# Attention inside a fused kernel: the value product with values stationary, and probabilities divided ahead of their transposes

## The chip, the cores and the metric

The kernel runs on one core of a Trainium2 chip. The metric is the device time of one execution in microseconds (us); lower is better. Engines are named as the profile names them: PE (matrix products; PEld is its weight loads), DVE, ACT and POOL (element-wise work), SP (issues most DMAs).

## What is computed

Three layers run one after another: chunked attention over 4 batches, 8 heads and 768 positions with 64 features per head; a two-layer network of width 2048; RMS normalisation and a gated two-layer network of width 1536. Only the attention is touched:

```
for each chunk of 32 queries (16 positions of left and 8 of right context, 8 memory slots):
    scores = (1/8) * q_chunk @ k_full.T          # k_full: 8 memory + up to 56 keys
    a = exp(scores - max);  a = a / (sum(a) + 1e-9)
    out_chunk = a @ v_full
x = out, tokens by 512 features (8 heads x 64)   # goes into the network after it
```

## The kernel before

The 3072 tokens are cut into 24 attention tiles of 128 tokens (four chunks of 32). Each tile goes through five steps, a PE part followed by the engine work that takes its result out of PSUM:

- **a** (L433, L445): 4 PE transposes of the queries (L438) and 4 of a key tile (L395); ACT and DVE copy them out.
- **b** (L453, L466): 32 score products, each 64 rows by 32 columns of the PE array, with 64 key columns moving (L458). In the trace each of these float32 products stands as two pairs of weight load and matmul, so a tile shows 64. DVE takes maxima (L471) and subtracts them (L472), ACT takes the exponentials (L477).
- **c** (L486, L495): 4 transposes of the probabilities (L490), copied out by ACT (L497).
- **d** (L501, L516): 32 value products (L506): the transposed probabilities are the stationary operand (32 queries), the values move, 64 features and a 65th column of ones, whose result is the sum. DVE adds the epsilon (L519), takes the reciprocal (L520) and multiplies (L522).
- **e** (L528, L535): the result has queries on partitions, and the next layer wants features there: 4 transposes (L532), copied by ACT (L539) into `xb`, which holds 384 tokens.

Scores and values share the PSUM pair `bkp`; all transposes rotate over two banks. `att_list` (L544) writes the steps of six tiles as a list with one step of lag between the letters: in each round e of tile t-4, d of t-3, c of t-2, b of t-1, a of t. The first list (tiles 0 to 5) runs at the start, with the conversion of the first weights (L202 to L216) put between its pieces; as soon as tile 2 has passed its last step (L976), `x_split` makes the first operands T out of `xb` and the first main products (L639 to L641, 384 columns each) begin to be put in. The lists for tiles 6 to 23 are spread over the slots between main products (`slots`, L990). Within this program order a scheduler fixes the order on each engine, and each engine then runs its own order strictly.

The values are loaded by SP (L379) as rows of 64 floats into `vw`, whose rows are 65 floats apart; raw weights for the conversion are loaded by POOL's queue (L149) into two buffers, so that POOL waits there until DVE has read the older one (L210). POOL also copies memory values (L385) and, later, adds for the main products (L669).

Of the kernel before, what the change touches and what calls it, by code (L numbers as in the profile page):

```python
# [8 lines left out]
F32 = mybir.dt.float32  # L9
# [4 lines left out]
ALU = mybir.AluOpType  # L14
AX = mybir.AxisListType

EPS_RMS = 1e-6
EPS_SUM = 1e-9
# [11 lines left out]
def tile_kernel(  # L30
# [15 lines left out]
    nc = tc.nc  # L46
    pin = tc.keep_in_program_order
    B, H, S, D = q.shape
    NMEM = mem_k.shape[2]
# [4 lines left out]
    NP = H // 2  # L54
# [269 lines left out]

    rot = [0]
    qn, kn, vn, ktw, qT, pt, pT = {}, {}, {}, {}, {}, {}, {}
    vw = [atp.tile([128, NP, 4, D + 1], F32, tag=f"vw{u}", name="vw") for u in range(2)]
    kw2 = [atp.tile([128, NP, 4, 64], F32, tag=f"kw{u}", name="kw") for u in range(2)]

    SMALL = [(2 * a + e, c) for a in range(NP) for c in range(4) for e in range(2)]  # L330

    def bank():
        rot[0] = (rot[0] + 1) % 2
        return bk[4 + rot[0]]
# [26 lines left out]
    def load_v(t):  # L361
        b, i = divmod(t, SPB)
        s0 = 128 * i
        vt = vw[t % 2]
        vn[t] = vt
        for h2 in range(2):
            p0 = 64 * h2
            if i < 2:
                src = mem_v[b].rearrange("(a e) s d -> e s a d", e=2)[h2]
                nc.sync.dma_start(out=vt[p0:p0 + NMEM, :, 3, 0:D], in_=src)  # L370
            for c in range(4):
                lo = 16 if i == 0 and c == 0 else 0
                hi = 48 if i == SPB - 1 and c == 3 else 56
                src = bass.AP(
                    v.tensor,
                    v.offset + ((b * H + h2) * S + s0 + 32 * c + lo - 16) * D,
                    [[D, hi - lo], [2 * S * D, NP], [1, D]],
                )
                nc.sync.dma_start(out=vt[p0 + NMEM + lo:p0 + NMEM + hi, :, c, 0:D], in_=src)  # L379

    def mem_v_copy(t):
        if t % SPB < 2:
            vt = vn[t]
            for p0 in (0, 64):
                nc.gpsimd.tensor_copy(  # L385
                    vt[p0:p0 + NMEM, :, 0:3, :],
                    vt[p0:p0 + NMEM, :, 3:4, :].to_broadcast([NMEM, NP, 3, D + 1]),
                )

    def k_pe(b, i):  # L390
# [75 lines left out]
    def att_b1(t):  # L466
        i = t % SPB
        ps = st_b.pop(t)
        mx = at2.tile([128, 2, NP], F32, tag="mx", name="mx")
        p = at1.tile([128, NP, 2, 64], F32, tag="p", name="p")  # L470
        nc.vector.reduce_max(mx, ps, axis=AX.X)  # L471
        nc.vector.tensor_tensor(  # L472
            p.rearrange("p a e k -> p e a k"), ps,
            mx.unsqueeze(3).to_broadcast([128, 2, NP, 64]), op=ALU.subtract
        )
        p = p.rearrange("p a e k -> p (a e) k")
        nc.scalar.activation(p, p, ACTF.Exp, scale=scale)  # L477
        if i == 0:
            nc.vector.memset(p[0:32, :, 8:24], 0.0)
        if i == SPB - 1:  # L480
            nc.vector.memset(p[96:128, :, 56:64], 0.0)
        pt[t] = p

    st_c, st_d, st_e, xs_t, xb = {}, {}, {}, {}, {}

    def att_c(t):  # L486
        p = pt.pop(t)
        pp = bank().rearrange("p (a s) -> p a s", a=NP)
        for a in range(NP):
            nc.tensor.transpose(  # L490
                pp[:, a, :], p[:, 2 * a:2 * a + 2, :].rearrange("s h d -> s (h d)"), ident
            )
        st_c[t] = pp

# [5 lines left out]

    def att_d(t):  # L501
        w, vt = pT.pop(t), vn[t]
        px = bk2[:, :, 0:NP * (D + 1)].rearrange("p e (a d) -> p e a d", a=NP)
        for h, c in SMALL:
            p0 = 64 * (h % 2)
            nc.tensor.matmul(  # L506
                px[32 * c:32 * c + 32, h % 2, h // 2, :],
                w[p0:p0 + 64, h // 2, 32 * c:32 * c + 32],
                vt[p0:p0 + 64, h // 2, c, :],
                tile_position=(p0, 32 * c),  # L510
            )
        st_d[t] = px
        if t + 2 < TSUB:
            load_v(t + 2)

    def att_d1(t):  # L516
        px = st_d.pop(t)
        sm = at2.tile([128, 2, NP], F32, tag="sm", name="sm")
        nc.vector.tensor_scalar_add(sm, px[:, :, :, D], EPS_SUM)  # L519
        nc.vector.reciprocal(sm, sm)  # L520
        x = at1.tile([128, NP, 2, D], F32, tag="x", name="x")
        nc.vector.tensor_tensor(  # L522
            x.rearrange("p a e d -> p e a d"), px[:, :, :, 0:D],
            sm.unsqueeze(3).to_broadcast([128, 2, NP, D]), op=ALU.mult
        )
        xs_t[t] = x

    def att_e(t):  # L528
        x = xs_t.pop(t)
        px = bank().rearrange("p (a s) -> p a s", a=NP)  # L530
        for a in range(NP):
            nc.tensor.transpose(px[:, a, :], x[:, a, :, :].rearrange("p e d -> p (e d)"), ident)  # L532
        st_e[t] = px

    def att_e1(t):  # L535
        n, r = divmod(t, NSUB)
        if r == 0:
            xb[n] = atx.tile([128, KC, N], F32, tag="xb", name="xb")
        nc.scalar.copy(xb[n][:, :, 128 * r:128 * r + 128], st_e.pop(t))  # L539

    att_ops = {"a": att_a, "a1": att_a1, "b": att_b, "b1": att_b1,
               "c": att_c, "c1": att_c1, "d": att_d, "d1": att_d1, "e": att_e, "e1": att_e1}

    def att_list(j):  # L544

        out = []
        t0 = TPP * j
        for s in range(TPP + 4):
            for op, lag in (("e", 4), ("d", 3), ("c", 2), ("b", 1), ("a", 0)):
                t = t0 + s - lag  # L550
                if t0 <= t < t0 + TPP:
                    if op == "a" and t % SPB == 0:
                        out.append([(att_a0, t)])
                    out.append([(att_ops[op], t), (att_ops[op + "1"], t)])
        return out
# [372 lines left out]
    make_identity(nc, ident)  # L928
    for x in vw:
        nc.gpsimd.memset(x, 0.0)  # L930
        nc.gpsimd.memset(x[:, :, :, D:D + 1], 1.0)
    nc.gpsimd.memset(ones, 1.0)
    nc.scalar.copy(ones_r, ones)

# [28 lines left out]
    for n, piece in enumerate(first):  # L963
        if n == 2:
            load_v(0)
        if n == 6:
            load_v(1)
        if n == 4:
            load_q(3)
        if n == 4:  # L970
            cv_prefetch(0)
        for fn, t in piece:
            fn(t)
        if n >= 4:
            cv_upto(CV_START * (n + 1 - 4) // (len(first) - 4))
        if piece[0] == (att_e, NSUB - 1):  # L976
            for half in range(2):
                x_split(0, half)
            heads, at_head = [unit(0, i) for i in range(NHEAD)], n
        elif n - at_head in HEADS:  # L980
            if next(heads[0], "end") == "end":
                heads.pop(0)
                next(heads[0])
# [304 lines left out]
```

## Time and profile before

| | |
|---|---|
| median of 3 runs | 1166.92 us (1166.48 to 1168.05) |
| the profiled execution | 1167.72 us, its span 1166.0 us |
| PE busy / PE weight loads busy | 1140.7 us (98%) / 1005.2 us (86%) |
| DVE / ACT / POOL busy | 823.8 / 629.2 / 183.4 us |
| chain that ended last | PE 75%, DMA 9%, DVE 8%, ACT 5% |

The attention lies in the first 310 us of the span. A busy PE in this profile is counted from a matmul's start to its modelled end, so bursts of small products count as busy whatever they do. In the trace's rows a line number is that of the kernel before, and a tile's name (`bkp`, `T`, `x`) is the program's.

### The profile page before, as it was taken

The page shows a single profiled execution, that of the slowest core. Times are in us where ns is not written, and L with a number is a line of the kernel's source. Part 1 is how long each engine was busy: PE and PEld are TensorE (multiplying, and loading weights), DVE is VectorE, ACT ScalarE, POOL GpSimd, SP SyncE. Part 2 cuts the span into 40 slices and gives each one's busy share as a digit, 9 for nine tenths or more (in the row PEclk, how much of TensorE's full clock was granted, in tenths as well). Part 3 has the DMA queues.
Part 4 walks back from the last instruction along what each step waited for, and adds up shares of the span by engine and source line. Part 5 has one row for each costly group of instructions (what it writes and reads, how often), then busy time and mean ns, then how long its engine had stood idle before and what let it go on. Part 6 is the DMA issues. An engine that isn't in the chain of part 4 may idle for free.

```text
span 1166.0 us, 22910 instructions
## 1 busy us (share of the span) xinstructions
PE 1140.7 (98%) x9052; PEld 1005.2 (86%) x9052; DVE 823.8 (71%) x1254; ACT 629.2 (54%) x1008; POOL 183.4 (16%) x165
## 2 busy tenths in 40 slices
PE   5899999999999999999999999999999999999998
PEld 4799999999999888888878778888888888999998
DVE  3655798844745876866776765967896857888873
ACT  4566666543645896677775443544454423444441
POOL 3011231311132311010011121110211111000000
PEclk8899999999999999999999999999999999999999
DMA  9989799898488774594599398999898889655421
GB/s 195 187 219 224 191 300 260 240 297 284 170 302 290 255 225 144 188 354 157 195 375 409 123 349 316 355 407 359 312 363 356 329 283 319 180 160 145 145 91 37
DMA packets 213276, 294.20 MB, mean 252 GB/s; under 512 B 104240, under 2 KB 160560, under 8 KB 204336
## 3 DMA queue, kind: packets, MB, share of 16 engines
q1 hardware_dynamic: 210864, 284.34, 73.5%
q0 software_dynamic: 2304, 8.39, 2.3%
q8 instruction: 71, 1.16, 0.4%
q14 instruction: 37, 0.30, 0.1%
HBM read 181.80 MB, written 110.89 MB: 251 GB/s over the span
## 4 chain that ended last, share of the span: by engine, by line
PE 75%; DMA 9%; DVE 8%; ACT 5%; issue 2%; POOL 0%; SPq 0%; ACTq 0%; DVEq 0%; POOLq 0%
PE bk L639 13%; PE bk L640 13%; PE bk L641 13%; DMA s<-g_scratch 4%; PE bk L912 4%; PE bk L914 4%; PE bk L913 4%; PE bk L755 3%; PE bk L756 3%; PE bk L754 3%; DVE T L154 2%; PE bkp L639 2%; PE bkp L640 2%; PE bkp L641 2%; PE bkp L506 2%
## 5 line engine op out<-in xcount | busy, mean ns | idle before, releaser
L639 PE MATMUL bk<-T,w 128*128 128x384 f32 (+1 forms) x860 | 315.6, 369 | 1.3 <-ACT c L657 1.0
L640 PE MATMUL bk<-T,w 128*128 128x384 f32 (+1 forms) x860 | 311.2, 362 | 0.0
L641 PE MATMUL bk<-T,w 128*128 128x384 f32 (+1 forms) x860 | 307.4, 361 | 0.0
L639 PEld LDWEIGHTS bk<-T,w 128*128 128x128 f32 x860 | 162.0, 189 | 21.0 <-ACT c L657 1.3
L640 PEld LDWEIGHTS bk<-T,w 128*128 128x128 f32 x860 | 161.9, 188 | 16.5 <-DVE T L154 0.3
L641 PEld LDWEIGHTS bk<-T,w 128*128 128x128 f32 x860 | 161.5, 188 | 15.8
L912 PE MATMUL bk<-w,T 128*128 128x256 f32 x396 | 112.1, 283 | 0.2 <-ACT T L153 0.2
L913 PE MATMUL bk<-w,T 128*128 128x256 f32 x396 | 112.0, 283 | 0.0
L914 PE MATMUL bk<-w,T 128*128 128x256 f32 x396 | 111.9, 283 | 0.0
L755 PE MATMUL bk<-T,w 128*128 128x512 f32 x276 | 107.5, 390 | 0.5 <-DVE T L154 0.5
L756 PE MATMUL bk<-T,w 128*128 128x512 f32 x276 | 107.1, 389 | 0.0
L754 PE MATMUL bk<-T,w 128*128 128x512 f32 x276 | 105.8, 389 | 0.0
L669 POOL TENSOR_TENSOR v<-c,v 128x512 f32<-128x512 f32 x36 | 54.1, 1503 | 291.7 <-DVE c L665 259.0
L665 DVE TENSOR_TENSOR c<-bk,c 128x512 f32<-128x512 f32 (+2 forms) x72 | 43.0, 598 | 54.5 <-PE bk L641 41.9
L912 PEld LDWEIGHTS bk<-w,T 128*128 128x128 f32 x396 | 76.0, 192 | 0.5 <-ACT T L153 0.4
L913 PEld LDWEIGHTS bk<-w,T 128*128 128x128 f32 x396 | 76.0, 192 | 0.0
L914 PEld LDWEIGHTS bk<-w,T 128*128 128x128 f32 x396 | 75.9, 192 | 0.0
L649 ACT COPY c<-bk 128x512 f32<-128x512 f32 (+2 forms) x72 | 36.9, 514 | 69.1 <-PE bk L641 25.3
L154 DVE TENSOR_TENSOR T<-s,T 128x1024 fp32r<-128x1024 f32 (+1 forms) x50 | 62.5, 1258 | 15.2 <-ACT T L153 15.1
L782 ACT ACTIVATE s<-s 128x1024 f32<-128x1024 f32 x44 | 46.4, 1059 | 31.3 <-DMA s<-g_scratch 31.2
L755 PEld LDWEIGHTS bk<-T,w 128*128 128x128 f32 x276 | 51.8, 188 | 11.6 <-DVE T L154 0.9
L756 PEld LDWEIGHTS bk<-T,w 128*128 128x128 f32 x276 | 51.8, 188 | 10.8
(228 smaller groups left out, 2284.6 us busy)
## 6 DMA issues: line engine op xcount, KB each, us to landing
T<-nt_scratch SPq DMA_DIRECT2D x35, 1024.0 KB
g_scratch<-g SPq DMA_DIRECT2D x64, 384.0 KB
s<-g_scratch SPq DMA_DIRECT2D x46, 512.0 KB
h_scratch<-s SPq DMA_DIRECT2D x36, 512.0 KB
w<-wg SPq DMA_DIRECT2D x10, 1792.0 KB
wg<-w SPq DMA_DIRECT2D x30, 512.0 KB
raw<-in_moe_w_out_dram SPq DMA_DIRECT2D x28, 512.0 KB
nt_scratch<-T SPq DMA_DIRECT2D x14, 1024.0 KB
```

The source lines that it names most:

```text
L154: keep((eng or nc.vector).tensor_tensor(lo, src, hi.bitcast(F32), op=ALU.subtract))
L639: nc.tensor.matmul(ps, whi, xh, start=first and kk == 0, stop=False, **more)
L640: nc.tensor.matmul(ps, whi, xl, start=False, stop=False, **more)
L641: nc.tensor.matmul(ps, wlo, xh, start=False, stop=kk == 1, **more)
L669: nc.gpsimd.tensor_tensor(c22, u3, z5, op=ALU.add)
L754: nc.tensor.matmul(ps, ahi, bhi, start=start, stop=False)
L755: nc.tensor.matmul(ps, ahi, blo, start=False, stop=False)
L756: nc.tensor.matmul(ps, alo, bhi, start=False, stop=stop)
L782: nc.scalar.activation(x, g, self.act)
L912: nc.tensor.matmul(ps, t[:, 0, f], w[:, 0], start=first and f == 0, stop=False, **more)
L913: nc.tensor.matmul(ps, t[:, 0, f], w[:, 1], start=False, stop=False, **more)
L914: nc.tensor.matmul(ps, t[:, 1, f], w[:, 0], start=False, stop=f == HG - 1, **more)
```

## The change

The value product swaps its operands. Values become stationary, in halves of 32 features (64 keys by 32 features), and the transposed probabilities move, 32 queries at a time. The result leaves with features on partitions, the layout that `xb` wants, so step e (its 4 transposes, its pass through PSUM) is gone and ACT copies the product straight into `xb`. A product now has 32 moving columns instead of 65, and a tile has 64 of them instead of 32. The column of ones is gone, and rows of `vw` are 64 floats apart. The sum is taken from the probabilities by DVE, and the probabilities are divided ahead of step c: on DVE for tiles 0 to 5, on POOL after that. A list has 25 pieces instead of 31.

```diff
-    vw = [atp.tile([128, NP, 4, D + 1], F32, tag=f"vw{u}", name="vw") for u in range(2)]
+    vw = [atp.tile([128, NP, 4, D], F32, tag=f"vw{u}", name="vw") for u in range(2)]
+    NFIRST = 6
+    VALUES = [(a, c, cols) for a in range(2) for c in range(4) for cols in range(4)]
...
     def att_b1(t):
...
-        pt[t] = p
+        sm = at2.tile([128, H], F32, tag="sm", name="sm")
+        nc.vector.reduce_sum(sm, p, axis=AX.X)
+        nc.vector.tensor_scalar_add(sm, sm, EPS_SUM)
+        nc.vector.reciprocal(sm, sm)
+        pn = at1.tile([128, NP, 2, 64], F32, tag="x", name="x")
+        mul = nc.vector if t < NFIRST else nc.gpsimd
+        mul.tensor_tensor(
+            pn.rearrange("p j r k -> p r j k"), p.rearrange("p (r j) k -> p r j k", r=2),
+            sm.rearrange("p (r j) -> p r j", r=2).unsqueeze(3).to_broadcast([128, 2, NP, 64]),
+            op=ALU.mult,
+        )
+        pt[t] = pn
...
     def att_d(t):
         w, vt = pT.pop(t), vn[t]
-        px = bk2[:, :, 0:NP * (D + 1)].rearrange("p e (a d) -> p e a d", a=NP)
-        for h, c in SMALL:
-            p0 = 64 * (h % 2)
-            nc.tensor.matmul(
-                px[32 * c:32 * c + 32, h % 2, h // 2, :],
-                w[p0:p0 + 64, h // 2, 32 * c:32 * c + 32],
-                vt[p0:p0 + 64, h // 2, c, :],
-                tile_position=(p0, 32 * c),
-            )
+        px = bk2[:, :, 0:256].rearrange("p e (a s) -> p e a s", a=2)
+        for a, c, cols in VALUES:
+            for e in range(2):
+                o = 32 * cols
+                j, d0 = 2 * a + cols // 2, 32 * (cols % 2)
+                p0 = 64 * e
+                nc.tensor.matmul(
+                    px[o:o + 32, e, a, 32 * c:32 * c + 32],
+                    vt[p0:p0 + 64, j, c, d0:d0 + 32],
+                    w[p0:p0 + 64, j, 32 * c:32 * c + 32],
+                    tile_position=(p0, o),
+                )
...
-    def att_e(t):
...
-    def att_e1(t):
...
-        nc.scalar.copy(xb[n][:, :, 128 * r:128 * r + 128], st_e.pop(t))
+        nc.scalar.copy(
+            xb[n].rearrange("p (e a) n -> p e a n", e=2)[:, :, :, 128 * r:128 * r + 128], st_d.pop(t)
+        )
...
-        for s in range(TPP + 4):
-            for op, lag in (("e", 4), ("d", 3), ("c", 2), ("b", 1), ("a", 0)):
+        for s in range(TPP + 3):
+            for op, lag in (("d", 3), ("c", 2), ("b", 1), ("a", 0)):
...
-        if piece[0] == (att_e, NSUB - 1):
+        if piece[0] == (att_d, NSUB - 1):
             for half in range(2):
                 x_split(0, half)
```

What the scheduler makes of it is shown at three places. In the rows of the change the lines are those of the changed kernel: L397 keys, L440 queries, L460 scores, L503 probability transposes, L522 values, L638 to L640 main products.

PE in the start of the program, from the keys of tile 5 (`kn`) to the first main product; before:

```order
L395 MATMUL bk_87<-ident,kn 128x128 x4
L458 MATMUL bkp<-kw,qT 32x64 x32
L532 MATMUL bk_86<-ident,x 128x128 x4
L506 MATMUL bkp<-vw,pT 32x65 x32
L490 MATMUL bk_87<-ident,p 128x128 x4
L438 MATMUL bk_86<-ident,qn 128x128 x4
L458 MATMUL bkp<-kw,qT 32x64 x32
L395 MATMUL bk_87<-ident,kn 128x24 x4
L532 MATMUL bk_86<-ident,x 128x128 x4
L506 MATMUL bkp<-vw,pT 32x65 x32
L490 MATMUL bk_87<-ident,p 128x128 x4
L639 MATMUL bk_82<-T,w 128x384
```

The same place with the change:

```order
L397 MATMUL bk_86<-ident,kn 128x128 x4
L522 MATMUL bkp<-pT,vw 32x32 x64
L503 MATMUL bk_87<-ident,x 128x128 x4
L440 MATMUL bk_86<-ident,qn 128x128 x4
L460 MATMUL bkp<-kw,qT 32x64 x32
L638 MATMUL bk_82<-T,w 128x384
L639 MATMUL bk_82<-T,w 128x384
```

The first main product now follows the scores of tile 4 directly; the values of tile 3, the transposes of tile 4 and the last, short key tile, which stood ahead of it, come behind.

DVE after the scores of tile 0 (`mx` maxima, `p` probabilities); before:

```order
L471 TENSOR_REDUCE mx<-bkp 128x8
L472 TENSOR_TENSOR p<-bkp,mx 128x2x4x64
L404 COPY kw<-bk_87 128x4x24
L479 MEMSET p 32x8x16
L471 TENSOR_REDUCE mx<-bkp 128x8
L472 TENSOR_TENSOR p<-bkp,mx 128x2x4x64
```

With the change:

```order
L473 TENSOR_REDUCE mx<-bkp 128x8
L474 TENSOR_TENSOR p<-bkp,mx 128x2x4x64
L406 COPY kw<-bk_87 128x4x24
L481 MEMSET p 32x8x16
L485 TENSOR_REDUCE sm<-p 128x8
L486 TENSOR_SCALAR sm<-sm 128x8
L487 RECIPROCAL sm<-sm 128x8
L490 TENSOR_TENSOR x<-p,sm 128x2x4x64
L473 TENSOR_REDUCE mx<-bkp 128x8
```

Four operations stand between the exponentials of a tile and its transposes, and ahead of the maxima of the next tile.

POOL where tiles 6 to 8 come (`raw` raw weights, `vw` values); before:

```order
L149 DMA raw<-in_moe_w_in_dram 128x2x512 x4
L385 COPY vw<-vw 8x4x195
L149 DMA raw<-in_moe_w_in_dram 128x2x512
L385 COPY vw<-vw 8x4x195 x3
L149 DMA raw<-in_moe_w_in_dram 128x2x512 x8
```

With the change:

```order
L149 DMA raw<-in_moe_w_in_dram 128x2x512 x4
L387 COPY vw<-vw 8x4x192 x2
L149 DMA raw<-in_moe_w_in_dram 128x2x512 x2
L387 COPY vw<-vw 8x4x192 x2
L490 TENSOR_TENSOR x<-p,sm 128x2x4x64
L149 DMA raw<-in_moe_w_in_dram 128x2x512 x2
L490 TENSOR_TENSOR x<-p,sm 128x2x4x64
L149 DMA raw<-in_moe_w_in_dram 128x2x512
L490 TENSOR_TENSOR x<-p,sm 128x2x4x64
```

The products with the reciprocal alternate with the issues of raw loads, which wait for a free buffer.

## Rows read from the trace of the kernel before

**Rows 1.** Stretches: us, busy by engine (instructions), granted clock, DMA share, GB/s.
```profile
0.00:40.00 40.00, 25.14 (x584) 18.25 (x584) 17.83 (x37) 20.99 (x40) 10.24 (x20) 0.83 0.93 193
40.00:50.00 10.00, 8.64 (x151) 7.65 (x136) 6.48 (x12) 5.76 (x11) 0.72 (x1) 0.83 0.97 193
50.00:70.00 20.00, 19.09 (x334) 17.04 (x319) 11.87 (x22) 12.52 (x25) 5.04 (x6) 1.00 0.87 193
70.00:220.00 150.00, 150.00 (x2282) 140.11 (x2270) 117.94 (x226) 95.63 (x186) 31.27 (x37) 1.00 0.88 237
230.00:310.00 80.00, 80.00 (x1143) 74.67 (x1142) 42.54 (x81) 33.94 (x64) 8.66 (x8) 1.00 0.78 251
```

**Rows 2.** Groups by line: busy us, mean ns of one | idle before, who ended it.
```profile
L669 POOL TENSOR_TENSOR v<-c,v 128x512 f32<-128x512 f32 x36 | 54.1, 1503 | 291.7 <-DVE c L665 259.0 <-ACT v L657 14.5 <-ACT s L747 12.0
...
L458 PE MATMUL bkp<-kw,qT 64*32 64x64 f32 x1536 | 24.4, 234 | 0.8 <-DVE x L522 0.7
L506 PE MATMUL bkp<-vw,pT 64*32 64x65 f32 x1536 | 22.9, 229 | 2.3 <-DMA vw<-in_v_dram 1.0 <-POOL vw L385 1.0 <-DVE p L472 0.2
...
L471 DVE TENSOR_REDUCE mx<-bkp 128x8 f32<-128x512 f32 x24 | 16.5, 688 | 25.0 <-PE bkp L458 24.9
...
L532 PE MATMUL bk<-ident,x 128*128 128x128 f32 x96 | 15.2, 283 | 2.0 <-ACT qT L449 1.9
...
L520 DVE RECIPROCAL sm<-sm 128x8 f32<-128x8 f32 x24 | 4.8, 201 | 0.7
```

**Rows 3.** Timeline of PE around lone result transposes: start us, us, what, count.
```profile
252.50 0.33 PE L641 MATMUL bk<-T,w 128*128 128x384 f32 x1
252.67 0.34 PE L639 MATMUL bk<-T,w 128*128 128x384 f32 x1
252.85 0.60 PE L532 MATMUL bk<-ident,x 128*128 128x128 f32 x4
...
253.47 0.33 PE L641 MATMUL bk<-T,w 128*128 128x384 f32 x1
```

**Rows 4.** Timeline of PE around a lone values burst.
```profile
196.75 0.34 PE L641 MATMUL bk<-T,w 128*128 128x384 f32 x1
197.02 0.86 PE L506 MATMUL bkp<-vw,pT 64*32 64x65 f32 x64
...
198.09 0.34 PE L640 MATMUL bk<-T,w 128*128 128x384 f32 x1
```

**Rows 5.** The same view at 39 us: a scores burst at half the clock.
```profile
39.07 1.06 PE L458 MATMUL bkp<-kw,qT 64*32 64x64 f32 x64
```

**Rows 6.** A slice of that burst: us, busy (instructions), granted clock, DMA share, GB/s.
```profile
39.40:39.60 0.20, 0.20 (x35) 0.50 1.01 257
```

**Rows 7.** PE, started from 197.0 to 197.3: matmuls of the burst of Rows 4.
```profile
197.02 0.48 PE L506 MATMUL bkp<-vw,pT 64*32 64x65 f32 x33
```

**Rows 8.** PE weight loads of that burst that started from 197.4 to 197.6.
```profile
197.40 0.31 PEld L506 LDWEIGHTS bkp<-vw,pT 64*32 64x32 f32 x25
```

**Rows 9.** Timeline of PE ahead of the first main product.
```profile
40.85 0.66 PE L532 MATMUL bk<-ident,x 128*128 128x128 f32 x4 [0.37 <-ACT qT L449]
...
42.85 0.87 PE L506 MATMUL bkp<-vw,pT 64*32 64x65 f32 x50 [0.79 <-DMA vw<-in_v_dram]
...
44.42 1.63 PE L639 MATMUL bk<-T,w 128*128 128x384 f32 x4
```

**Rows 10.** Timelines of ACT and PE at tile 15: exponentials, then transposes.
```profile
186.17 0.63 ACT L477 ACTIVATE p<-p 128x512 f32<-128x512 f32 x1
...
186.85 0.66 PE L490 MATMUL bk<-ident,p 128*128 128x128 f32 x4
```

**Rows 11.** DMA queue of SP, 2.5:4.2 us, queries and keys: packets, MB, share of 16 engines.
```profile
q1 hardware_dynamic: 1248, 0.31, 80.9%
```

**Rows 12.** DMA queue of SP, 48:53 us, values: packets, MB, share of 16 engines.
```profile
q1 hardware_dynamic: 3431, 0.85, 124.4%
```

**Rows 13.** DMA queue of SP, 41.2:45.6 us, mostly values: packets, MB, share of 16 engines.
```profile
q1 hardware_dynamic: 1900, 0.46, 50.9%
```

More of the change, by code (lines that the diff above doesn't have):

```diff
@@ L368, in load_v @@
             if i < 2:
-                src = mem_v[b].rearrange("(a e) s d -> e s a d", e=2)[h2]
-                nc.sync.dma_start(out=vt[p0:p0 + NMEM, :, 3, 0:D], in_=src)
+                src = mem_v[b].rearrange("(e a) s d -> e s a d", e=2)[h2]
+                nc.sync.dma_start(out=vt[p0:p0 + NMEM, :, 3, :], in_=src)
             for c in range(4):
@@ L375, in load_v @@
                     v.tensor,
-                    v.offset + ((b * H + h2) * S + s0 + 32 * c + lo - 16) * D,
-                    [[D, hi - lo], [2 * S * D, NP], [1, D]],
+                    v.offset + ((b * H + NP * h2) * S + s0 + 32 * c + lo - 16) * D,
+                    [[D, hi - lo], [S * D, NP], [1, D]],
                 )
-                nc.sync.dma_start(out=vt[p0 + NMEM + lo:p0 + NMEM + hi, :, c, 0:D], in_=src)
+                nc.sync.dma_start(out=vt[p0 + NMEM + lo:p0 + NMEM + hi, :, c, :], in_=src)
     def mem_v_copy(t):
@@ L386, in mem_v_copy @@
                     vt[p0:p0 + NMEM, :, 0:3, :],
-                    vt[p0:p0 + NMEM, :, 3:4, :].to_broadcast([NMEM, NP, 3, D + 1]),
+                    vt[p0:p0 + NMEM, :, 3:4, :].to_broadcast([NMEM, NP, 3, D]),
                 )
@@ L481, in att_b1 @@
             nc.vector.memset(p[96:128, :, 56:64], 0.0)
-        pt[t] = p
-    st_c, st_d, st_e, xs_t, xb = {}, {}, {}, {}, {}
+        sm = at2.tile([128, H], F32, tag="sm", name="sm")
[10 more added lines that the diff above has]
+        pt[t] = pn
+    st_c, st_d, xb = {}, {}, {}
     def att_c(t):
@@ L490, in att_c @@
             nc.tensor.transpose(
-                pp[:, a, :], p[:, 2 * a:2 * a + 2, :].rearrange("s h d -> s (h d)"), ident
+                pp[:, a, :], p[:, a].rearrange("s h d -> s (h d)"), ident
             )
@@ L516, in att_d1 @@
     def att_d1(t):
[L517 to L526, printed above, removed]
-    def att_e(t):
[L529 to L533, printed above, removed]
-    def att_e1(t):
         n, r = divmod(t, NSUB)
@@ L538, in att_e1 @@
             xb[n] = atx.tile([128, KC, N], F32, tag="xb", name="xb")
-        nc.scalar.copy(xb[n][:, :, 128 * r:128 * r + 128], st_e.pop(t))
+        nc.scalar.copy(
+            xb[n].rearrange("p (e a) n -> p e a n", e=2)[:, :, :, 128 * r:128 * r + 128], st_d.pop(t)
+        )
     att_ops = {"a": att_a, "a1": att_a1, "b": att_b, "b1": att_b1,
-               "c": att_c, "c1": att_c1, "d": att_d, "d1": att_d1, "e": att_e, "e1": att_e1}
+               "c": att_c, "c1": att_c1, "d": att_d, "d1": att_d1}
     def att_list(j):
@@ L930, in tile_kernel @@
         nc.gpsimd.memset(x, 0.0)
-        nc.gpsimd.memset(x[:, :, :, D:D + 1], 1.0)
     nc.gpsimd.memset(ones, 1.0)
```

## The prediction

> **What bounds the kernel now.** Read first the table of stretches [rows 1]. From 70 to 220 us PE is busy 150.00 of 150.00 us, from 230 to 310 us 80.00 of 80.00, while DVE has 117.94 of 150. There a microsecond of PE work, added or removed, is a microsecond of the total, and other engines matter only where they make PE wait. The start is different: PE is busy 25.14 of the first 40 us, 8.64 of the next 10 and 19.09 of the 20 after them, 17.1 us of idle in all, with DMA at 0.93 and 0.97; the granted clock averages 0.83 there, 2.4 GHz with stretches of 1.2. There the order of loads and the length of the chain decide. Then the groups by line [rows 2], for prices; then timelines around single pieces [rows 3 to 10], because busy time of overlapped bursts doesn't tell what a burst costs PE's stream. The profiled execution took 1167.7 us, 0.8 above the median of 1166.9; I work out differences and put them on the median.
>
> **Step e goes (24 times).** Around a lone set of result transposes, main products start at 252.50, 252.67, then 252.85 for the transposes, and 253.47 for the second product behind them [rows 3]. An ordinary step is 0.17; from 252.67 to 253.47 there are two steps and the transposes, so a set costs 0.80 - 0.34 = 0.46 us. 24 x 0.46 = 11.0 us less.
>
> **Step d doubles its instructions (24 times).** A lone burst of 64 stands between the products at 196.75 and 198.09 [rows 4]: 1.34 - 0.34 = 1.00 us now. With the change it is 128 pairs, each with 32 moving columns instead of 65. No row shows such a burst, so I bound its extra cost.
> Near the bottom: is the pace set by columns? A scores burst of the same 64 took 1.06 us [rows 5] in a slice where the clock was 0.50, the level of 1.2 GHz [rows 6], against 0.86 at full clock [rows 4]. Halving the clock added 0.20, so at most about 0.20 of the 0.86 hangs on columns. A matmul's own run is 0.23 [rows 2]. The remaining 0.86 - 0.20 - 0.23 = 0.43 goes with the number of instructions and doubles: +0.43. (If pace went by columns alone it would be +0, but these rows speak against it.)
> From the pace: the first 33 matmuls of the burst cover 0.48 us [rows 7], or 32 starts in 0.48 - 0.23 = 0.25, 8 ns each. The other 31 need 0.86 - 0.48 = 0.38, 12 ns each: +0.78 for 64 more at that pace. Within that slower half the weight loads run 25 in 0.2 us, 8 ns each [rows 8], and only its two ends are slow. I take 0.52 (64 at 8.2), since a longer burst has the same ends once. 24 x 0.52 = 12.5 us more; bounds 10.3 and 18.7.
> [...]
>
> **The start.** Before the change, the first main product stands at 44.42 [rows 9], behind the result transposes of tile 2 (40.85), the values of tile 3, whose rest waited for a load until 42.85, and the transposes of tile 4. In the new order it stands right behind the scores of tile 4, which end at 39.07 + 1.06 = 40.1 [rows 5]: up to 4.3 us earlier. Not all of it is gain. What PE no longer does ahead of it (d of tile 3 at 1.00; c of tile 4, three sets of e and a short key tile, as five sets of transposes at 0.46: 3.3 us) it partly does later, and the three value bursts that stay are 0.52 longer, so work ahead falls by about 1.7 and idle by about 2.6. I take 2.5 us less; bounds 0 (DMA sets the end of the start anyway: share 0.87 to 0.97 up to 70 us [rows 1], and the value loads of tiles 4 and 5 still follow the old bursts) and 4.3. SP's own queue issues the same loads; only the queries of tile 6 change places with the values of tile 3.
>
> **The division moves ahead of c.** DVE keeps the addition and the reciprocal (0.20 [rows 2]) and gains a sum over 128x512, no dearer than the maxima (0.69 [rows 2]); for tiles 0 to 5 it keeps the product too (as many elements as the maxima, 0.69), from tile 6 POOL has it, priced at 1.50 by the nearest 128x512 product on POOL [rows 2]. DVE's total stays within 4 us and is not the bound. But the chain from exponentials to transposes grows by 0.69 + 0.20 + 0.20 + 1.50 = 2.6 us. Cover: the new order puts more between scores and transposes. At tile 15 there are 25 main products instead of 17, the value burst is 0.52 longer, one key transpose more, the e set gone: 1.4 + 0.5 + 0.1 - 0.46 = +1.6. In the trace before, the exponentials of tile 15 end at 186.17 + 0.63 = 186.80 and the transposes start at 186.85 [rows 10]: no slack. So PE would wait 2.6 - 1.6 = 1.0 there. Behind the waiting transposes stand all main products, and nobody else can use PE. Tiles 14 to 17 and 23 have similar distances, the others some 2 us more; I take 1.5 us in all, bounds 0 and 4. Where the sum or the product comes late, the next to wait are ACT's copy of the transposes and the values.
>
> ACT keeps its count: one copy of 128x512 out of PSUM per tile leaves with e and one comes with d, and `bkp` is now freed by that copy instead of by three DVE operations; I cost this at nothing, since before the change scores waited on that release 0.7 us in all [rows 2].
>
> **Sum.** -11.0 + 12.5 - 2.5 + 1.5 = +0.5 us: 1166.9 + 0.5 = 1167.4 (a profiled execution near 1168.2). It is a trade of transposes for instructions that comes out even. What a measurement here can tell from no change is about 0.2%, 2.3 us.
>
> **Rivals.**
> *Faster, the start pays in full* (chance 0.24): the whole 4.3 us holds, no transposes wait, and the burst costs its lower bound: -11.0 + 10.3 - 4.3 = -5.0, 1161.9. For it: DMA-bound starts shorten by any load made lighter. At 48 to 53 us, with value loads alone, a packet of 256 B took 1.244 x 16 x 5 us / 3431 = 29 ns [rows 12], query and key packets 0.809 x 16 x 1.7 / 1248 = 17.6 ns [rows 11]; value rows will lie 256 B apart instead of 260. Against it: in another stretch of value loads it is 0.509 x 16 x 4.4 / 1900 = 18.9 ns with the same 260 [rows 13], so the distance is not shown to be the cause. If all value packets fell to 17.6, a tile's 1792 would save up to 1.3 us of all 16 engines, and the end would be near 1160.
> [...]
> *Slower, the burst runs at its slow pace throughout* (0.20): 12 ns for each further pair: -11.0 + 18.7 - 2.5 + 1.5 = +6.7, 1173.6. It decides from 9.5 ns a pair on. For it: half of today's burst averages that.
> *Slower, POOL's product is the new wait* (0.14): it is queued behind issues of raw loads that wait for a buffer, or takes over 2 us; from about 1 us beyond my price, tiles 14 to 17 and 23 wait 2 us each instead of 0.3 and several others begin to: about +10, 1177.
>
> **How the numbers follow.** The forecast has 0.42 and a spread of some 3 us on both sides (the start, the waits): 0.34 of it within 2.3 us of 1166.9, 0.02 faster, 0.06 slower. With the first rival faster has 0.26, with the two others slower 0.40. The likeliest case's own range is 1164 to 1171; for 8 in 10 the range is 1161 to 1176, which leaves out the full lighter loads and the worst of the POOL waits.
>
> **What would show it.** In the changed profile: no 128x128 transposes of `x` as results; value bursts of 128 matmuls that last 1.3 to 1.4 us (1.6 or more: the slow pace; 1.0 or less: columns set it); the first main product near 40 us; PE idle in 0 to 70 us near 14.5 instead of 17.1; a POOL product of about 1.5 us; PE idle before probability transposes in tiles 14 to 17 of about 1 us. Wrong it is if bursts cost under 1.2 or over 1.7 us, if the first main product doesn't move, or if PE idles over 4 us between 70 and 310 us.

## The result, and the profile after

The changed kernel takes 1184.74 us (median of 4 runs, 1183.71 to 1186.03) against 1167.49 of the kernel before beside it (1166.48 to 1168.64): ratio 1.0148, 95% interval 1.013 to 1.0166, 17 us slower. The forecast was 1167.4 and the range ended at 1176. The profiled execution has a span of 1183.0 us against 1166.0.

The page's busy line and its row of the second DMA queue, first of before, then of after:

```profile
PE 1140.7 (98%) x9052; PEld 1005.2 (86%) x9052; DVE 823.8 (71%) x1254; ACT 629.2 (54%) x1008; POOL 183.4 (16%) x165
...
q8 instruction: 71, 1.16, 0.4%
```

```profile
PE 1148.2 (97%) x10492; PEld 1012.0 (86%) x10492; DVE 834.4 (71%) x1260; ACT 627.4 (53%) x1008; POOL 206.0 (17%) x181
...
q8 instruction: 82, 1.34, 0.5%
```

PE has 1440 matmuls and as many weight loads more (+1536 for values, -96 transposes), and queue q8, which brings instructions, carries 82 packets instead of 71. 2 x 10492 / 82 = 256 and 2 x 9052 / 71 = 255: a packet is a block of about 256 PE instructions, 1.34 MB / 82 = 16.3 KB each. The mean granted clock is 0.993 in both profiled executions.

The stretches of [rows 1], after:

```profile
0.00:40.00 40.00, 24.50 (x698) 18.79 (x699) 20.82 (x43) 18.85 (x36) 10.48 (x18) 0.91 0.90 191
40.00:50.00 10.00, 9.04 (x225) 7.41 (x223) 7.33 (x15) 6.21 (x11) 0.72 (x1) 0.86 0.83 158
50.00:70.00 20.00, 16.98 (x386) 15.50 (x387) 10.23 (x22) 11.29 (x23) 3.76 (x5) 0.83 0.84 195
70.00:220.00 150.00, 145.31 (x2697) 133.97 (x2695) 115.81 (x205) 91.54 (x178) 42.61 (x44) 1.00 0.81 223
230.00:310.00 80.00, 77.29 (x1398) 70.34 (x1398) 40.32 (x76) 32.28 (x61) 18.55 (x17) 1.00 0.86 274
```

Idle of PE in the first 70 us is 19.5 us instead of 17.1 (forecast 14.5), and 4.7 and 2.7 us have appeared in two stretches that had none (over 4 us there was a sign of being wrong by the prediction's own words). What PE waited for, from the waits of PE over the whole span (total us, times, longest):

```profile
PE bkp L522 <- issue: 6.6, 4, 3.4
...
PE bk L503 <- POOL x L490: 4.0, 3, 1.7
PE bk L640 <- issue: 2.5, 2, 1.3
PE bk L503 <- DVE x L490: 2.1, 2, 1.3
```

None of the four is in the same view of before. "issue" means that the engine waited for nothing that the profile shows. Three pieces of PE's timeline show where these stand, beside a value burst that runs through:

```profile
27.80 0.41 PE L522 MATMUL bkp<-pT,vw 64*32 64x32 f32 x23
31.58 0.43 PE L522 MATMUL bkp<-pT,vw 64*32 64x32 f32 x20 [3.37 <-issue]
...
57.31 0.85 PE L522 MATMUL bkp<-pT,vw 64*32 64x32 f32 x72
60.40 0.72 PE L522 MATMUL bkp<-pT,vw 64*32 64x32 f32 x41 [2.23 <-issue]
...
102.20 0.34 PE L640 MATMUL bk<-T,w 128*128 128x384 f32 x1
102.47 1.41 PE L522 MATMUL bkp<-pT,vw 64*32 64x32 f32 x128
103.81 0.45 PE L638 MATMUL bk<-T,w 128*128 128x384 f32 x1
...
264.88 0.33 PE L639 MATMUL bk<-T,w 128*128 128x384 f32 x1
266.38 0.34 PE L640 MATMUL bk<-T,w 128*128 128x384 f32 x1 [1.16 <-issue]
```

PE stops in the middle of a burst that has read the same operands already, or between two main products of one accumulation. Count PE's records from the start, matmuls, weight loads and the semaphore instructions of its sequencer together. Then five of the six "issue" waits, those that begin at 28.21, 58.16, 231.77, 265.21 and 279.58 us, end with records 962, 2242, 8642, 9666 and 10178. Each number is 194 modulo 256 (the remainder after division by 256): always the edge of a block. They sum to 8.3 us. The sixth, 0.74 us at 26.15, stands ahead of a burst's first product and at no edge; the trace doesn't show its cause.

The packets on q8 fit. There are 82 such edges and 82 packets. Paired in order, the first packet with the second edge, up to 340 us no block is entered less than 1.28 us after its packet's end, and at the five stops PE goes on 1.28 to 1.60 us after it: the packet of the second stop runs from 57.63 to 59.10, and PE goes on at 60.39. Half of the packets start within 1.2 us after PE enters the block before, but PE enters one at 260.21 and the next packet runs only from 264.16 to 265.10; PE stands until 266.38. The kernel before crosses such edges 71 times, with packets just as late (PE enters a block at 100.13, the packet starts at 103.97), and up to 340 us it has no stop at an edge: its blocks last 5.1 us and more. Now one value burst alone, 128 matmuls and 128 weight loads, is a whole block in 1.4 us, and the blocks ahead of the stops at 28, 58, 265 and 279 us were used up in 3.1 to 5.4 us. A short block is not enough by itself: one of 3.64 us (21.21 to 24.85), whose packet started 1.2 us after PE entered it, brought no stop.

The second stop is followed by a slow stretch:

```profile
60.40:66.60 6.20, 6.20 (x61) 5.89 (x61) 3.08 (x7) 3.84 (x8) 2.17 (x3) 0.50 0.49 125
```

At this granted clock of 0.50 main products start 0.32 us apart instead of 0.17. Over the whole execution the clock was the same as before the change (0.993), so it does not explain the 17 us; only the place of the slow stretches differs. For the prediction's 2.4 GHz the traces show 2.4 columns per ns at a clock of 1.00: main products of 256 columns start 3.12 / 26 = 0.120 us apart (1139.79 to 1142.91, before), those of 512 columns 4.08 / 18 = 0.227 (699.81 to 703.89, after), 0.107 us more for 256 more columns; its 1.2 is half of that, at 0.50.

This is what the sections below test: blocks of 256 instructions, one packet of 16.3 KB each on q8, of which 77 of the 82 edges bring no "issue" wait, and the other five cost 8.3 us.

### The profile page after: what moved, and what is told of

Read it like the earlier page. It is cut to its first block, busy times and chain, and to the rows that moved or that the text cites. A ratio compares the mean times of both kernels' runs of the same rounds, so it can differ in the third digit from the quotient of the medians.

```text
span 1183.0 us, 25858 instructions
## 1 busy us (share of the span) xinstructions
PE 1148.2 (97%) x10492; PEld 1012.0 (86%) x10492; DVE 834.4 (71%) x1260; ACT 627.4 (53%) x1008; POOL 206.0 (17%) x181
## 3 DMA queue, kind: packets, MB, share of 16 engines
q8 instruction: 82, 1.34, 0.5%
## 4 chain that ended last, share of the span: by engine, by line
PE 76%; DVE 9%; DMA 6%; ACT 6%; issue 3%; POOL 1%; SPq 0%; ACTq 0%; DVEq 0%; POOLq 0%
PE bk L638 13%; PE bk L640 13%; PE bk L639 13%; PE bk L913 4%; PE bk L912 4%; PE bk L911 4%; PE bk L754 3%; PE bk L755 3%; PE bk L753 3%; DMA s<-g_scratch 2%; PE bkp L522 2%; PE bkp L638 2%; PE bkp L640 2%; PE bkp L639 2%; DMA T<-nt_scratch 2%
## 5 line engine op out<-in xcount | busy, mean ns | idle before, releaser
L638 PE MATMUL bk<-T,w 128*128 128x384 f32 (+1 forms) x860 | 316.4, 370 | 1.5 <-DMA T<-nt_scratch 0.6
L640 PE MATMUL bk<-T,w 128*128 128x384 f32 (+1 forms) x860 | 309.0, 362 | 2.5 <-issue 2.5
L638 PEld LDWEIGHTS bk<-T,w 128*128 128x128 f32 x860 | 161.8, 188 | 23.2 <-issue 1.3
L640 PEld LDWEIGHTS bk<-T,w 128*128 128x128 f32 x860 | 161.9, 188 | 17.3 <-issue 1.6
L664 DVE TENSOR_TENSOR c<-bk,c 128x512 f32<-128x512 f32 (+2 forms) x72 | 43.1, 598 | 56.1 <-PE bk L640 45.6
L154 DVE TENSOR_TENSOR T<-s,T 128x1024 fp32r<-128x1024 f32 (+1 forms) x50 | 62.4, 1255 | 13.6 <-ACT T L153 13.4
```

The lines of the kernel that those rows point to most:

```text
L154: keep((eng or nc.vector).tensor_tensor(lo, src, hi.bitcast(F32), op=ALU.subtract))
L638: nc.tensor.matmul(ps, whi, xh, start=first and kk == 0, stop=False, **more)
L640: nc.tensor.matmul(ps, wlo, xh, start=False, stop=kk == 1, **more)
```

## The experiments

All are shown as ratio to the kernel before, run beside it on the same chip, with the 95% interval; the us with a sign are (ratio - 1) x 1167.5. Theories: F, instructions (longer bursts and stops at block edges); W, the division ahead of the transposes; P, V, B, Q and others as the expectations define them.

**cols64**: one value product over 64 features instead of two over 32.

```
-    VALUES = [(a, c, cols) for a in range(2) for c in range(4) for cols in range(4)]
+    VALUES = [(a, c, cols) for a in range(2) for c in range(4) for cols in range(2)]
...
-                o = 32 * cols
-                j, d0 = 2 * a + cols // 2, 32 * (cols % 2)
+                o = 64 * cols
+                j = 2 * a + cols
...
-                    px[o:o + 32, e, a, 32 * c:32 * c + 32],
-                    vt[p0:p0 + 64, j, c, d0:d0 + 32],
+                    px[o:o + 64, e, a, 32 * c:32 * c + 32],
+                    vt[p0:p0 + 64, j, c, :],
```

> The changed kernel with the values stationary as 64 keys x 64 features instead of two halves of 32: the same result layout and the same division, but 32 value products a tile instead of 64 (64 PE records a burst instead of 128). Theory F (instructions: more of them per burst, and PE standing still until its next block of 256 instructions is there): the 24 x 0.48 us of the bursts and nearly all of the 9.6 us of stillness inside bursts and between main products where the instruction number is 194 modulo 256 go: 1164 us (1161 to 1167). Theory W (the division ahead of the transposes is the cause): only the bursts' 11.5 us go, the rest stays: 1173. Theory C (half clock and loads at the start): idle of 0 to 70 us stays near 19 us.

Measured 1176.12 us, ratio 1.0074 (1.0053 to 1.0095): +8.6, half of the loss back. Of PE's waits:

```profile
PE bk L503 <- DVE x L490: 3.0, 4, 1.3
PE bk L503 <- POOL x L490: 2.9, 3, 1.1
...
PE bk L638 <- DVE c L664: 2.2, 3, 1.1
PE bk L638 <- ACT w L153: 1.3, 2, 0.8
PE bk L638 <- ACT c L656: 1.2, 1, 1.2
PE bk L638 <- ACT c L648: 1.2, 2, 0.7
```

"issue" has shrunk to 0.9, and that one stands at no block edge: this trace has no stop at an edge, as F says. But main products now wait for DVE and ACT, 5.9 us by the last four rows; the largest such row of these lines is 1.0 us before and 0.6 after the change. The burst is also dearer than I expected: 1.33 us between the main products around it (110.17 to 111.51), against 1.06 of the kernel before and 1.54 after, so it saves 0.2 us a tile, not 0.48. Neither theory's number is met.

**dve24**: `NFIRST = 24`, the product on DVE in every tile.

> The changed kernel with the division on DVE for all 24 tiles instead of the first 6 only. Theory F: only the waits of the probability transposes on POOL's product go (4.0 us, 3 times): 1181 us (1179 to 1183), the stops at instruction number 194 modulo 256 stay. Theory W: POOL's product is the larger cause, and what waits behind it goes too: 1175 or less.

1185.6 us, ratio 1.0156 (1.0133 to 1.018). Moving the product away from POOL gains nothing, so POOL's product is not the cause; both theories expected a gain. The "issue" waits are 9.4 us, against 9.1 in the change.

**b_split**: the kernel before, each value product cut in two along its moving columns.

```
+            for lo, hi in ((0, 32), (32, D + 1)):
                 nc.tensor.matmul(
-                    px[32 * c:32 * c + 32, h % 2, h // 2, :],
+                    px[32 * c:32 * c + 32, h % 2, h // 2, lo:hi],
...
-                    vt[p0:p0 + 64, h // 2, c, :],
+                    vt[p0:p0 + 64, h // 2, c, lo:hi],
```

> The kernel before with every value product cut into two, of 32 and 33 moving columns: twice the value instructions, everything else (step e, the division behind the product, the loads) as before. Theory F: 24 x 0.48 = 11.5 us for the bursts and 4 to 9 us of stillness at a constant instruction number modulo 256: 1167.5 + 15 to 20 = 1183 to 1188. Theory W: the bursts alone, 1179, and no gap of over 0.4 us inside a value burst.

1193.44 us, ratio 1.0218 (1.0196 to 1.0241): +25.5. Its bursts take 1.668 between main products, 0.61 more than the 1.060 of before: 24 x 0.61 = 14.6. Its waits:

```profile
PE bkp L507 <- issue: 8.8, 5, 3.1
...
PE bkp L458 <- issue: 1.5, 2, 0.8
...
PE bk L640 <- issue: 0.7, 1, 0.7
PE bk L642 <- issue: 0.6, 1, 0.6
```

14.6 + 11.6 = 26.2. Ten stops of 0.4 us and more stand at block edges (194 modulo 256 again), 12.1 us in all, one of them put down to DVE by the view; the kernel before has none. Doubling the value instructions in the old kernel, where nothing else is changed, brings the stops: F is shown here. The sum fits better than its terms: by the page PE's busy time grew by 18.0 us (1158.7 against 1140.7) and its idle time by 7.1, because other waits became shorter.

**b_early**: the kernel before with the division ahead of the transposes, all products and step e as they were.

```
+        sm = at2.tile([128, H], F32, tag="sm", name="sm")
+        nc.vector.reduce_sum(sm, p, axis=AX.X)
+        nc.vector.tensor_scalar_add(sm, sm, EPS_SUM)
+        nc.vector.reciprocal(sm, sm)
+        mul = nc.vector if t < 6 else nc.gpsimd
+        mul.tensor_tensor(p, p, sm.unsqueeze(2).to_broadcast([128, H, 64]), op=ALU.mult)
...
-            sm.unsqueeze(3).to_broadcast([128, 2, NP, D]), op=ALU.mult
-        )
+        nc.vector.tensor_copy(x.rearrange("p a e d -> p e a d"), px[:, :, :, 0:D])
```

> The kernel before with the division moved ahead of the probability transposes (sum, addition, reciprocal and product there, on DVE for tiles 0 to 5 and on POOL from tile 6; behind the values DVE only copies), all products and step e as before. Theory F: only waits of the probability transposes on the product, 2 to 6 us: 1170 to 1173, no stops at a constant instruction number. Theory W: 1177 or more.

1186.35 us, ratio 1.0161 (1.0138 to 1.0185): +18.8. W's number. The waits are not at the transposes (1.8 us for the product) but mostly spread over ACT's and DVE's other work:

```profile
PE bk L438 <- ACT xb L539: 3.1, 3, 1.4
PE bk L639 <- ACT g L691: 2.5, 1, 2.5
PE bk L639 <- ACT T L153: 1.9, 2, 1.0
PE bk L640 <- issue: 1.8, 1, 1.8
...
PE bk L641 <- DVE w L154: 1.7, 1, 1.7
```

The "issue" wait of 1.8 us, at 274.44, is a stop at a block edge (194 modulo 256), with a packet that started 4.6 us after PE entered the block before: a late packet can stop PE without doubled instructions too, here once. So each suspect alone costs as much on the kernel before as the whole change does, or more. The next four take the division apart, and away.

**b_sum** (only the sum, addition and reciprocal early) and **b_mul** (only one product by ones ahead of the transposes):

> The kernel before with the sum, the addition and the reciprocal moved to right behind the exponentials on DVE; the product with the reciprocal stays behind the values, all else as before. The early division as a whole cost 18.4 us on the kernel before. Theory D (DVE works in order: its sum waits for ACT's exponentials at the head of the queue and holds up what DVE does for the main products): most of it is here already, 1178 us or more. Theory L (what costs is the longer way from scores to the transposes of the probabilities): that way is not longer here, 1171 or less.

> The kernel before with one product of 128x512 by ones put between the exponentials and the transposes (on DVE for tiles 0 to 5, on POOL from tile 6); the real division stays behind the values. Theory D: DVE waits for nothing new from tile 6 on, 1171 us or less. Theory L: the way to the transposes is 1.3 us longer plus the hand-overs, with more work than before on no other engine, 1174 or more, with PE waiting for POOL's product ahead of the transposes.

b_sum 1175.46, ratio 1.0078 (1.0051 to 1.0104), +9.1; b_mul 1171.95, ratio 1.0043 (1.0028 to 1.0058), +5.0. Both fall between the numbers of D and L: each part costs, the sum more by the medians, and together (18.8) more than the two apart (14.1).

**nodiv** and **c64_nodiv**: the changed kernel, and cols64, without any division (the lines from `sm = ...` to the product go, and the transposes read `p`).

> The changed kernel without any division (sum, addition, reciprocal and product are left out, so the rows are not normalised and the heads stand in another order); the value products in halves of 32 stay. Theory F (blocks of instructions): 8 to 9 us of lost time stay, 1176 us or more. Theory W (the division ahead of the transposes): the lost time goes but for the start, 1172 or less.

> The same without division, and with the value products over 64 features as in the run before of that kind: neither of the two suspects is left, so what remains is the gain of the missing result transposes: 1167.9 - 10.4 = 1157.5 us by both theories. Over 1162 there is a third cause in the change (the layout, the loads, the copy behind the values).

nodiv 1183.36, ratio 1.0141 (1.0115 to 1.0167); c64_nodiv 1170.86, ratio 1.0025 (1.001 to 1.004). As a square, in us over before:

```
                     with division   without
halves of 32             +17.3        +16.5
64 features               +8.6         +2.9
```

The halves cost 8.7 us with the division and 13.6 without it. In the changed kernel the division is nearly free: without it its waits go, and the stops grow. Those of nodiv:

```profile
PE bkp L511 <- issue: 5.3, 4, 2.3
PE bkp L460 <- issue: 4.6, 4, 2.0
...
PE bk L627 <- issue: 2.0, 2, 1.4
```

11.9 us where the change itself has 9.1; at block edges 10.6 against 8.3. And c64_nodiv, with neither suspect, does not gain: the 10 us of the transposes are missing. Its burst of 1.33 us explains a part, which the expectation left out: 24 x (1.33 - 1.06) = 6.5 us. The other 7 were a third question.

**b_noe**: the kernel before without the 96 result transposes.

```
-        px = bank().rearrange("p (a s) -> p a s", a=NP)
-        for a in range(NP):
-            nc.tensor.transpose(px[:, a, :], x[:, a, :, :].rearrange("p e d -> p (e d)"), ident)
-        st_e[t] = px
+        st_e[t] = x.rearrange("p a e d -> p a (e d)")
```

> The kernel before without the 96 transposes of the results (ACT copies the rows as they stand, so features are not on partitions); DVE, ACT and POOL do as much as before. Theory P (as the prediction had it: PE sets the pace from 70 to 310 us): 24 x 0.46 us off, 1156 us. Theory V (DVE, busy 29 of 30 us in some stretches before the change, takes over as soon as PE has less to do): only a part of it, 1160 to 1166 us, with main products that wait for DVE or ACT.

1170.10 us, ratio 1.0022 (1.001 to 1.0035). P's 1156 is out of reach: taking the work away gives nothing. The stretch from 120 to 190 us, of before and then of b_noe (columns as in [rows 1]):

```profile
120.00:190.00 70.00, 70.00 (x1012) 65.15 (x1012) 63.89 (x119) 45.97 (x90) 18.41 (x21) 1.00 0.87 247
```

```profile
120.00:190.00 70.00, 66.32 (x974) 60.08 (x973) 63.55 (x116) 45.06 (x88) 18.12 (x21) 1.00 0.89 251
```

PE idles 3.7 us of it, and 3.6 more than before in the first 70 us. Over the whole span its busy time fell by 7.6 us (1133.1 against 1140.7) and its idle time grew by 6.9. Main products (L636 here) now wait for ACT and DVE, the longest of these waits by total:

```profile
PE bk L636 <- ACT w L153: 1.7, 2, 1.1
PE bk L636 <- DVE c L651: 1.3, 2, 1.0
PE bk L636 <- ACT T L153: 1.3, 1, 1.3
```

The mean of DVE in [rows 1], 117.94 of 150 us, hid that it is busy 29.05 of the 30 us from 160 to 190 in the same trace. Whether that is what holds PE up is the question of the next runs.

**c64_nomax, after_nomax, b_nomax**: no maximum and no subtraction, the exponentials straight from PSUM, which lightens DVE.

```
-        nc.vector.reduce_max(mx, ps, axis=AX.X)
...
-        nc.scalar.activation(p, p, ACTF.Exp, scale=scale)
+        nc.scalar.activation(p.rearrange("p a e k -> p e a k"), ps, ACTF.Exp, scale=scale)
```

> The changed kernel with value products over 64 features, and without the row's maximum and its subtraction (ACT takes the exponentials from PSUM), which is some 1.37 us less of DVE in each of 24 tiles; division, transposes and values as in the run of 64 features before (1176). Theory V: DVE's load is what turned 10 us of gain into a loss, so most of it comes back: 1157 to 1161. Theory F or one of the chain's length alone: 1170 or more, less some 2 us for the shorter chain.

> The changed kernel, values in halves of 32, without the maximum and its subtraction. Theory V with F: DVE's part of the loss goes, the stops for blocks of instructions stay: 1166.9 + 1.1 + 8.5 = 1176 us (1173 to 1179). Theory V alone: 1168. Theory F alone: 1183.

> The kernel before without the maximum and its subtraction, a control for the two others. PE never waits from 70 to 310 us before the change, so by theories P and V alike only the start can gain: 1163 to 1167 us.

c64_nomax 1173.41 (1.0041, 1.0026 to 1.0056), after_nomax 1185.20 (1.0148, 1.0134 to 1.0161), b_nomax 1173.78 (1.0052, 1.004 to 1.0064). Against V: 1.37 us less of DVE in each of 24 tiles gives cols64 back 3.8 us at best, the change nothing, and makes the kernel before slower. after_nomax shows the exchange once more: its waits on the division are down to 0.6 us, its "issue" waits up to 13.9:

```profile
PE bkp L516 <- issue: 6.8, 7, 3.0
PE bkp L460 <- issue: 5.0, 5, 1.5
...
PE bk L633 <- issue: 1.3, 1, 1.3
PE bk L634 <- issue: 0.8, 1, 0.8
```

**b_noe_max16, b_max16, after_max16**: `reduce_max(mx, ps[:, :, :, 0:16])`, one DVE operation shorter and no order touched. **b_noe_t6**: b_noe from tile 6 on.

> As b_noe (the kernel before without result transposes), with the row's maximum taken over 16 of the 64 keys: one DVE operation a tile of some 0.2 instead of 0.69 us, at the same place, with the same hand-overs. Theory V (DVE's load in 120 to 180 us took the gain): the 4 to 5 us lost there come back, 1165 us (1163 to 1167) where b_noe had 1170. Theory Q (the order in which ACT, DVE and PE hand work to each other, not how much there is): 1169 to 1172.

> The kernel before with the maximum over 16 of 64 keys, the control. PE does not wait from 70 to 310 us, so by theory V nothing changes but perhaps the start: 1164 to 1168. Theory Q: any shift of a hand-over costs, 1169 or more.

> The changed kernel with the maximum over 16 of 64 keys. Theory V: DVE reaches the sum and the reciprocal 0.5 us earlier in each tile, so the waits of the probability transposes (4.0 + 2.1 us) nearly go: 1179 to 1181. Theory Q: 1183 or more. The stops at instruction number 194 modulo 256 stay by both.

> As b_noe, but the result transposes are left out only from tile 6 on (18 of 24 sets); the first six stay. Theory S (the start is bound by loads, and takes the gain of the first six sets): the same time as b_noe, 1170 (1168 to 1171). Theory P (each set is worth its 0.43 us): 2.6 us more than b_noe, 1172 to 1173.5.

b_noe_max16 1169.08 (1.0008, 0.999 to 1.0026), b_max16 1172.32 (1.0029, 1.0017 to 1.0042), after_max16 1185.97 (1.0147, 1.0126 to 1.0167), b_noe_t6 1169.04 (1.0008, 0.9998 to 1.0019). V's numbers fail, Q's hold; that a shorter operation alone costs 3.4 us on the kernel before (and b_nomax 6.1) I can't explain. So less work on DVE alone made the kernel before slower by that much; a difference of that size on it, b_mul's 5.0 among them, shows no cause by itself. In after_max16 the waits on the division fall from 6.1 to 2.5 us and the "issue" waits rise to 11.8. b_noe_t6 equals b_noe: the start gives nothing for its six sets, and the other 18 give nothing either.

**b_2e**: the kernel before with each result transpose done twice (`for again in range(2)` around it). **c64_empty**: cols64 with an empty piece of work where step e stood.

> The kernel before with every result transpose done twice into the same place: 96 transposes more on PE, nothing else. Theory B (PE and the chain between ACT and DVE are close together: work added on PE counts in full, work taken away does not, since the other chain then sets the pace): 24 x 0.43 = 10 us more, 1178 us (1176 to 1180), although the same 96 taken away gave nothing. If a set is worth little in both directions (PE's work overlaps with waits that the trace doesn't show): 1172 or less.

> The changed kernel with value products over 64 features, and with an empty piece of work wherever step e stood, so that all other pieces keep the places among the main products that they had before the change. If the places (fewer, wider spaced pieces; the first main product earlier) cost the time: 1168 to 1171 us where the same kernel without empty pieces had 1176. If the division and its hand-overs do: 1174 to 1179.

b_2e 1177.88, ratio 1.009 (1.0073 to 1.0106): +10.5, B's number. The same 96 transposes cost 10.5 us added and return nothing taken away. One thing was not equal: the granted clock of b_2e's executions is 0.995 to 0.999, that of the kernel beside it 0.993 to 0.996, so the price may be a little higher. c64_empty 1179.06, ratio 1.0102 (1.0088 to 1.0117): the places of the pieces are not what cols64 loses by.

None of these versions is faster than the kernel before.

## Why the prediction was wrong, point by point

**Step d, +12.5.** The price of the burst was right: 1.539 us between main products against 1.060, 0.48 each, 24 x 0.48 = 11.5. It ran at 0.48 / 64 = 7.5 ns a pair, a little below the 8.2 of the forecast and far from the rival's 12. The pace of a pair is not what made the change slower.

**The term that was missing.** The sum priced instructions by their time on PE and had none for bringing them in. This is the first of two steps that failed (the other is step e, below): 8.3 us of stops at block edges (5.6 of it at 28 and 58 us, ahead of and in the stretch that the forecast wanted shorter). That doubled instructions cause them is shown by b_split (12.1 us, the old kernel) and by the four kernels with 64 features, which have no stop at an edge. Counted in the same way, all six traces with doubled value instructions have 5 to 12 such stops, 8.3 to 13.2 us; of the other fourteen only b_early has one. A row was there to count from: 71 packets on q8 for 2 x 9052 instructions.

**The division, +1.5, bounds 0 and 4.** The waits sum to 6.1 us. Tile 15, the one worked out, from the timelines of DVE, ACT, POOL and PE:

```profile
199.63 0.68 DVE L474 TENSOR_TENSOR p<-bkp,mx 128x512 f32<-128x512 f32 x1
...
200.52 0.65 ACT L479 ACTIVATE p<-p 128x512 f32<-128x512 f32 x1
...
201.20 0.69 DVE L485 TENSOR_REDUCE sm<-p 128x8 f32<-128x512 f32 x1 [0.42 <-ACT p L479]
201.80 0.41 DVE L209 TENSOR_SCALAR ca<-ca 128x512 int32<-128x512 int32 x1
202.13 0.16 DVE L486 TENSOR_SCALAR sm<-sm 128x8 f32<-128x8 f32 x1
202.25 0.69 DVE L210 SCALAR_TENSOR_TENSOR ca<-raw,ca 128x512 int32<-128x512 int32 x1
202.86 0.20 DVE L487 RECIPROCAL sm<-sm 128x8 f32<-128x8 f32 x1
...
203.22 1.29 POOL L490 TENSOR_TENSOR x<-p,sm 128x512 f32<-128x512 f32 x1 [5.39 <-DVE sm L487]
...
204.57 0.44 PE L503 MATMUL bk<-ident,x 128*128 128x128 f32 x2 [1.73 <-POOL x L490]
```

From the end of the exponentials (201.17) to the transposes it is 3.4 us, not 2.6. The operations have the durations that I gave them (POOL's product 1.29, less than 1.50), but two operations of the weight conversion, L209 and L210, stand between sum, addition and reciprocal on DVE. I had added up durations of one engine's work as if it were in one piece. Yet what this cost the changed kernel is small: nodiv has no division and is nearly as slow.

**The start, -2.5.** The first main product came at 43.16, 1.3 us earlier than [rows 9], not 4.3; idle to 70 us grew by 2.4. Two stops (3.37 and 2.23) and the 2.1 us on DVE's product, which the sum had left out for tiles 0 to 5, are more than that.

**Step e, -11.0.** This is the second step that failed: -11.0 forecast, and +2.6 measured where the transposes alone are taken away (b_noe). "A microsecond of PE work, added or removed, is a microsecond of the total" was half right. Added it is, as far as the totals show (b_2e +10.5; b_split in the sum). Removed it is not (b_noe, b_noe_t6): main products then wait for conversions and sums by ACT and DVE. PE at 150.00 of 150.00 [rows 1] told that PE never waited, not how far behind it the others were; 117.94 of 150 on DVE looked like room, but PE and DVE work in turn for each other, and b_noe shows PE idle 3.7 us of 70 as soon as it has less to do.

**The sum over.** With 10.5 for the transposes (b_2e) and the rows of after: -10.5 + 11.5 + 9.1 + 6.1 = 16.2, against 17.3 measured. That it comes so near is partly luck. By the page PE's busy time grew by 7.5 us, where the first two terms give 1.0, and its idle time by 9.5 (span less busy, 34.8 against 25.3), where the last two give 15.2. So 5.7 us of other waits have gone, and 6.5 us of busy time have no term; which work took them is open. The terms aren't independent either: with the waits on the division gone the stops grow (nodiv, after_nomax, after_max16: 11.8 to 13.9 us), with the stops gone others appear (cols64). The five kernels with halves of 32 (the change, dve24, nodiv, after_nomax, after_max16) took 1183 to 1186 us; the four with 64 features 1171 to 1179. The doubled instructions are what sets the changed kernel apart from these four; that is shown. Without them and without the division the kernel is still 2.9 us slower than before (c64_nodiv): the gain of step e never came. Of the rivals none came true: the start gained no 4.3 us, the pace was faster than the slow one, and POOL's product, though PE waited 4.0 us for it, is no cause (dve24).

Left open: which hand-over between ACT and DVE takes up the room that the missing transposes leave (a lighter DVE did not free it), why b_max16 and b_nomax are slower, and why some block packets start 4 us after PE enters the block before. A value burst cut in two halves with main products between them, which would spread a block over more time, was not tried.

## What to carry to other kernels

Before you split products into more instructions, divide PE's instructions by the packets on the instruction queue and look at how long PE takes for that many where they are densest, and at how late the packets start: here blocks used up in 3.1 to 5.4 us brought stops of up to 3.4 us when their packets came late, and the kernel before, whose shortest lasts 5.1 us, had none. An engine that is busy 100% was here a price list for what was added (96 transposes, +10.5 us), not for what was taken away (the same 96, +2.6 us); to learn the second, take the work away in an experiment before building the change that pays for it. And add up a chain with whatever its engines have queued between its links: at tile 15 it took 3.4 us, where the durations of its own operations had been added up to 2.6.

## What was not expected of the hardware

- Blocks of 256 PE instructions that come late: up to 3.37 us of idle inside one burst, always at one remainder modulo 256, and ended 1.28 to 1.60 us after the block's packet.
- 64 pairs with 64x64 tiles and 32 moving columns take longer (1.33 us between main products) than 64 pairs with 64x32 tiles and 65 columns (1.06).
- Bursts with the same 128 pairs are not the same: 1.54 with values stationary, 1.67 with probabilities stationary and 32 or 33 columns.
